# Two banks for the last expert's two halves, and the order lists of a fused attention, gMLP and MoE kernel rewritten

## The chip, the cores and the metric

One core of one Trainium2 chip runs the whole program. The metric is the device time of one execution in microseconds (us); every time below is of that kind or read from one profiled execution. Engines are called as in the profile: PE multiplies matrices (PEld is its loading of weights), DVE is the vector engine, ACT the scalar engine, POOL the general engine, SP the engine that issues most of the transfers.

## What is computed

Three stages, each on the output of the one before, in float32:

```python
# 1. attention, 8 heads, S = 768, D = 64: a key is seen by a query of the same LSH bucket only
q_bucket = bits of (q @ proj > 0); k_bucket = bits of (k @ proj > 0)      # 6 bits
scores = where(q_bucket == k_bucket, q @ k.T / sqrt(D), -1e9)
attn = exp(scores - max); attn = attn / (sum(attn) + 1e-9); out = attn @ v
# 2. gMLP on x [768, 512], d_ff = 1024
h = gelu(x @ w_in); u, v = halves of h
v_n = (v - mu) / sqrt(var + 1e-6) * g_ln
x = x + (u * (w_sg @ v_n + b_sg)) @ w_out
# 3. sticky mixture of 8 experts: each token goes to one expert, its own best one
#    or, where a gate says so, that of the token before
out[s] = p[e] * (relu(x[s] @ w1[e]) @ w2[e])                              # 512 -> 1024 -> 512
```

## The kernel before, in words

**One program, four lists.** The order of every engine's work is written out by hand. Four texts hold it: `ATTENTION` (563 entries), `FEED_FORWARD` (133), `MIXING` (447) and `EXPERTS` (366). `_order` (L165) splits a text into entries of a name and numbers, "*2" meaning twice. A loop over each list (L653, L975, L1029, L1150) calls the step that the name stands for, and each step issues its instructions on its engines. So the place of an entry sets, for each engine that it uses, what stands ahead of it in that engine's queue; an engine takes its queue in order, and a wait at its head holds up all that is behind.

**ATTENTION.** The steps for a head h and a query tile i: `score` (PE, L456 and L459: q times k, and the penalty of the buckets), `max` (DVE, L463), `exp` (ACT, L467), `turn` (PE transposes 128x128 blocks of the numerators, L474), `ev` (ACT copies them to SBUF as `pt`, L480), `pv` (PE, `po<-pt,vt`, L490). `fetch`, `prep` (POOL L404, L405, L215; DVE L398, L384), `project` (PE L440) and `bits` (DVE L447, L449) make q, k and buckets of a head two or one ahead; `prep` also sends pieces through SP (`b<-q`, L399). `vt 0` issues the transfer of all of v into `vt` from ACT's queue (L638); `sum_v` and `pv` read it. `conv` and, later, `cv` are one chunk each of a conversion of the weights w_in and w_out from 64-bit words (`f64_chunks`, `cv_a`, `cv_w`).

**FEED_FORWARD.** `h n t` multiplies row tile t of x with half n of w_in (12 matmuls, L317); n = 1 is the half v. `sq`, `cub`, `tanh`, `gelu` (ACT L753, L757; DVE L755, L764) make the gelu; for the v half `dev`, `var`, `z`, `norm` (DVE L767, L772, L774; ACT L769, L777; POOL `rstd`, L775) make the layer norm, and `vh`, `vl` split it into a high and a low part `vn` (DVE L779, POOL L215). `wsg t i` reads a slice of w_sg (i = 2, SP), casts it (i = 0, ACT `wshi`, L791) and splits off the low part (i = 1, POOL `wslo`, L215, three instructions).

**MIXING.** `mix t k` are the multiplies of w_sg with `vn` for row tile t (L800), `gated` and `gT` and `out` the product with u and w_out; `res` adds the residual, `route` and `half`, `fill`, `rows` the routing. A copy into `route_bank` (DVE L987, ACT L988) stands at one place among them. Beside them run the reads of the experts' weights: 64 parts of 512 KB. `wr` issues the next read (SP, L700), `wh` casts it (ACT, L708), `wl` takes the difference as a low part (DVE, L718; POOL, L215, for 17 of the parts). Six tiles form the ring of the reads, so a read waits for the cast and the split of the part six before it.

**EXPERTS.** For each expert e: `g` and `gx` gather its tokens, `f` multiplies with w1 (L1078), `relu`, `ht` (turns), `y e j` with w2 (L1110, four matmuls per entry), `yo` weighs the sum with the token's probability (`weigh`, DVE L1118, or ACT L1120 for the last two experts), and `send` scatters the rows to the output (`scatter`, POOL, L1123). Experts 0 to 6 have a `y` of 512 columns in six entries. The last has its columns in two halves of six entries each (`cols_of`, L1099), so that the first half can be weighed while the second is multiplied. The sums of expert e lie in PSUM bank "m" or "v", in turn. `ext` (L1131) counts tokens that are left over.

Of the kernel before, what the change touches and what calls it, by code (L numbers as in the profile page):

```python
# [42 lines left out]
ev 1 0, prep 0 k1, prep 0 k2, sum_v 0 1, max 1 1, score 1 3, turn 1 3, exp 1 1, turn 0 6, project 1, sum 1 2,
max 1 3, ev 1 3, sum 1 0, sum_v 0 2, exp 1 3, bits 1 1, turn 1 1, score 1 4, bits 1 2, conv 0, score 1 5, ev 0 6,
sum_v 0 3, max 1 5, sum_v 0 4, sum_v 0 5, turn 1 4, ev 1 1, max 1 4, prep 1 q2, exp 1 5, exp 1 4, bits 1 0,
turn 1 2, ev 1 2, ev 1 4, fetch 2, pv 0 0, pv 0 1, conv 0, pv 0 2, pv 0 3, bits 1 3, sum 1 1, pv 0 4, score 2 0,
max 2 0, turn 1 5, score 2 1, turn 1 7, max 2 1, ev 1 5, exp 2 0, ev 1 7, mean_v 0, prep 1 lo, prep 1 k1, turn 1 8,
score 2 2, prep 1 k2, turn 1 6, exp 2 1, max 2 2, pv 0 5, score 2 3, ev 1 8, zt 0, conv 0, ev 1 6, turn 2 2,
exp 2 2, project 2, turn 2 3, ev 2 2, score 2 4, out 1, turn 2 1, max 2 3, bits 2 1, exp 2 3, ev 2 3, score 2 5,
turn 2 0, ev 2 1, max 2 4, sum 2 1, turn 2 5, conv 0, pv 1 0, ev 2 0, max 2 5, sum 2 0, conv 0, bits 2 2, pv 1 1,  # L50
bits 2 0, prep 2 q2, exp 2 4, ev 2 5, sum 1 3, pv 1 2, turn 2 4, bits 2 3, score 3 0, conv 0, max 3 0, exp 2 5,
score 3 1, max 3 1, prep 2 lo, turn 2 7, ev 2 4, mean 2, sum 3 0, sum 2 2, pv 1 3, fetch 3, pv 1 4, conv 0, ev 2 7,
turn 2 8, conv 0 *2, exp 3 0, score 3 3, turn 2 6, pv 1 5, exp 3 1, prep 2 k1, ev 2 8, conv 0, sum 2 3, ev 2 6,
prep 2 k2, max 3 3, out 2, fetch 4, exp 3 3, sum 3 1, to_x 2, score 3 2, turn 3 0, turn 3 1, mean 3, ev 3 0,
max 3 2, to_x 3, score 3 4, ev 3 1, exp 3 2, conv 0, max 3 4, turn 3 2, turn 3 5, project 3, score 3 5, pv 2 0,
ev 3 5, bits 3 2, pv 2 1, max 3 5, ev 3 2, bits 3 1, conv 0, pv 2 2, turn 3 4, exp 3 4, sum 3 2, exp 3 5, ev 3 4,
bits 3 0, prep 3 k1, turn 3 3, bits 3 3, sum 3 3, conv 0, score 4 0, prep 3 k2, sum 4 1, ev 3 3, turn 3 8, max 4 0,
turn 3 6, score 4 1, conv 0, ev 3 8, ev 3 6, conv 0, xT 3, exp 4 0, pv 2 3, prep 3 q2, pv 2 4, pv 2 5, max 4 1,
exp 4 1, low 3, score 4 2, turn 3 7, mean 4, sum 4 0, max 4 2, turn 4 0, out 3, prep 3 lo, to_x 4, ev 3 7, sum 4 2,
score 4 3, turn 4 2, ev 4 0, exp 4 2, conv 0, turn 4 1, project 4, score 4 4, max 4 3, conv 0, sum 4 3, exp 4 3,  # L60
bits 4 2, score 4 5, bits 4 0, bits 4 3, ev 4 2, turn 4 3, ev 4 1, max 4 4, tri 0, ev 4 3, bits 4 1, turn 4 4,
pv 3 0, max 4 5, pv 3 1, exp 4 4, pv 3 2, score 5 0, ev 4 4, exp 4 5, prep 4 k1, mean 5, prep 4 q2, xT 4, sum 5 1,
turn 4 5, turn 4 6, ev 4 6, max 5 0, score 5 1, prep 4 lo, pv 3 3, pv 3 4, max 5 1, conv 0, ev 4 5, pv 3 5, exp 5 0,
low 4, prep 4 k2, exp 5 1, turn 5 0, turn 4 8, out 4, score 5 2, max 5 2, conv 0, ev 5 0, to_x 5, ev 4 8, turn 4 7,
conv 0, sum 5 0, score 5 3, turn 5 1, project 5, max 5 3, conv 0, ev 4 7, exp 5 2, bits 5 2, fetch 5, score 5 4,
exp 5 3, conv 0, turn 5 2, score 5 5, ev 5 1, turn 5 3, pv 4 0, max 5 4, exp 5 4, bits 5 1, pv 4 1, ev 5 2,
bits 5 0, ev 5 3, conv 0, pv 4 2, max 5 5, turn 5 5, turn 5 4, conv 0, sum 5 2, score 6 0, exp 5 5, bits 5 3,
conv 0, ev 5 4, ev 5 5, conv 0, score 6 1, sum 6 0, sum 6 1, sum 5 3, turn 5 7, turn 5 6, conv 0, prep 5 q2, conv 0,
pv 4 3, pv 4 4, max 6 0, ev 5 7, exp 6 0, prep 5 k1, prep 5 lo, ev 5 6, pv 4 5, max 6 1, conv 0, exp 6 1, prep 5 k2,
score 6 2, xT 5, max 6 2, score 6 5, turn 5 8, conv 0, turn 6 1, conv 0, low 5, out 5, mean 6, pv 5 0, exp 6 2,  # L70
max 6 5, ev 5 8, pv 5 1, to_x 6, score 6 4, exp 6 5, conv 0, turn 6 2, score 6 3, conv 0, ev 6 1, ev 6 2, turn 6 3,
turn 6 0, project 6, pv 5 2, max 6 4, conv 0, max 6 3, bits 6 3, ev 6 0, bits 6 0, exp 6 4, bits 6 2, ev 6 3,
bits 6 1, conv 0, pv 5 3, exp 6 3, turn 6 7, turn 6 8, sum 7 2, sum 7 1, ev 6 7, conv 0, score 7 1, turn 6 4,
max 7 1, conv 0, score 7 0, max 7 0, pv 5 4, ev 6 8, ev 6 4, sum 7 0, exp 7 1, pv 5 5, score 7 4, conv 0, exp 7 0,
out 6, turn 6 5, conv 0, turn 6 6, conv 0, score 7 3, ev 6 5, sum 6 2, prep -1 hi, turn 7 0, max 7 4, sum 6 3,
conv 0, ev 6 6, sum 7 3, conv 0, exp 7 4, xT 6, conv 0, max 7 3, pv 6 0, pv 6 1, exp 7 3, score 7 2, ev 7 0,
max 7 2, score 7 5, turn 7 1, turn 7 2, pv 6 2, conv 0, ev 7 1, exp 7 2, ev 7 2, pv 6 3, conv 0, max 7 5, low 6,
pv 6 4, conv 0, exp 7 5, pv 6 5, turn 7 4, ev 7 4, mean 7, turn 7 7, conv 0, ev 7 7, conv 0, hv 0 0, sum 8 0,
turn 7 3, ev 7 3, conv 0, turn 7 6, hv 2 0, conv 0, ev 7 6, turn 7 8, conv 0, to_x 7, turn 7 5, mean 8, out 7,
sum 8 1, conv 0, ev 7 8, hv 0 1, conv 0, sum 8 2, hv 1 0, conv 0, ev 7 5, to_x 8, xT 7, low 7, pv 7 0, conv 0,  # L80
pv 7 1, conv 0 *2, pv 7 2, conv 0, sum 8 3, pv 7 3, pv 7 4, pv 7 5, conv 0, out 8, hv 3 0, conv 0, mean 9, xT 8,
to_x 9, hv 2 1, hv 1 1, conv 0, hv 0 2, xT 10, hv 1 2, low 8, xT 9, conv 0, hv 3 1, low 10, hv 2 2, hv 3 2, low 9
# [1229 lines left out]
```

## Time and profile before

| | us |
|---|---|
| runs | 343.32, 345.90, 342.52; median 343.32 |
| profiled execution, its own time | 342.49 |
| its span, first to last instruction | 340.7 |
| ATTENTION, to the last `po` | 136.4 |
| first multiply of `mix` | 167.9 |

A run's time has the profiled execution's span and about 1.8 us around it. Busy time is the time in which an engine worked on an instruction. A wait in square brackets in the timeline is the idle time of that engine just before the row's first instruction, with the work that ended it. Rows that follow one another with the same names are joined, with their count behind x.

### The profile page before, as it was taken

What the parts mean: (1) busy time and instruction counts of PE and PEld (TensorE: products, weight loads), DVE (VectorE), ACT (ScalarE), POOL (GpSimd) and SP (SyncE); (2) the same over time, 40 slices, a digit from 0 to 9 for tenths busy, and PEclk for the clock granted to TensorE, in tenths of its full rate; (3) what the DMA queues carried; (4) which work ended last, traced back from release to release, by engine and by line L of the source; (5) the groups of instructions that cost most, each with busy time, mean ns of one, the idle gap of its engine ahead of it and who ended that gap; (6) DMA issues with size and microseconds to landing.
All of it is one profiled execution on the core that took longest, in us unless ns stands there. A gap on an engine that the chain in (4) does not pass through costs nothing.

```text
span 340.7 us, 5610 instructions
## 1 busy us (share of the span) xinstructions
PE 323.5 (95%) x1842; PEld 253.9 (75%) x1842; DVE 263.9 (77%) x524; ACT 228.0 (67%) x403; POOL 216.9 (64%) x314
## 2 busy tenths in 40 slices
...
GB/s 239 52 327 144 196 70 200 117 69 64 202 68 86 64 62 141 63 160 10 2 169 109 201 108 300 158 188 231 360 252 333 350 350 313 285 341 315 282 29 31
DMA packets 27777, 59.97 MB, mean 176 GB/s; under 512 B 3230, under 2 KB 8094, under 8 KB 27744
## 3 DMA queue, kind: packets, MB, share of 16 engines
...
q0 software_dynamic: 1120, 3.15, 2.5%
...
## 4 chain that ended last, share of the span: by engine, by line
PE 39%; DVE 21%; DMA 18%; POOL 10%; issue 7%; ACT 2%; POOLq 1%; DVEq 0%; ACTq 0%
DMA out<-y,dst_row 12%; PE vs L800 7%; PE po L490 6%; DMA raw<-in_w 6%; PE t L474 4%; PE o L823 4%; DVE nb_all L463 3%; PE hv L317 3%; PE eh L1078 3%; POOL q L405 2%; PE s L456 2%; PE s L459 2%; DVE w L718 2%; POOL b L215 2%; POOL r L404 2%
## 5 line engine op out<-in xcount | busy, mean ns | idle before, releaser
L215 POOL TENSOR_TENSOR w<-raw,w 128x256 fp32r<-128x256 f32 x68 | 51.9, 796 | 35.1 <-ACT w L708 35.1
L708 ACT CAST w<-raw 128x1024 fp32r<-128x1024 f32 x64 | 65.4, 1055 | 12.4 <-DMA raw<-in_w 7.8
L718 DVE TENSOR_TENSOR w<-raw,w 128x1024 fp32r<-128x1024 f32 x47 | 57.1, 1253 | 5.1 <-ACT w L708 5.0
L467 ACT ACTIVATE e<-s,nb_all 128x768 f32<-128x768 f32 x48 | 43.5, 907 | 19.1 <-DVE nb_all L463 17.8
L463 DVE TENSOR_REDUCE nb_all<-s 128x1 f32<-128x768 f32 x48 | 45.5, 953 | 9.5 <-PE s L459 8.8
L480 ACT COPY pt<-t 128x512 f32<-128x512 f32 x72 | 40.3, 588 | 10.5 <-PE t L474 10.1
L474 PE MATMUL t<-ident,e 128*128 128x128 f32 x288 | 39.8, 274 | 0.5 <-ACT pt L480 0.4
L474 PEld LDWEIGHTS t<-ident,e 128*128 128x128 f32 x288 | 33.7, 140 | 7.0 <-issue 2.3
L490 PE MATMUL po<-pt,vt 128*64 128x384 f32 x192 | 34.7, 495 | 0.0
L1110 PE MATMUL y<-w,hh 128*128 128x512 f32 (+1 forms) x144 | 33.5, 371 | 0.6 <-ACT y L1120 0.6
L456 PE MATMUL s<-k,q 128*128 128x384 f32 x96 | 28.2, 374 | 0.9 <-ACT e L467 0.9
L1110 PEld LDWEIGHTS y<-w,hh 128*128 128x128 f32 x144 | 24.6, 188 | 4.9 <-ACT y L1120 0.8
L800 PE MATMUL vs<-vn,wshi 128*128 128x512 f32 x72 | 24.9, 407 | 1.9 <-ACT wshi L791 1.9
L459 PE MATMUL s<-k,q 76*128 76x384 f32 x96 | 25.5, 344 | 1.1 <-DVE q L447 0.8
L1123 POOL DMA_INDIRECT out<-y,dst_row x8 | 10.1, 1262 | 25.3 <-DVE y L1118 11.9
L1078 PE MATMUL eh<-w,xh 128*128 128x512 f32 x96 | 24.8, 397 | 0.1
L490 PEld LDWEIGHTS po<-pt,vt 128*64 128x64 f32 x192 | 12.3, 136 | 14.3 <-issue 14.1
L215 POOL TENSOR_TENSOR b<-r,k 64x256 fp32r<-64x256 f32 x21 | 15.9, 784 | 9.9 <-DVE k L384 9.8
L317 PE MATMUL h<-w_in_s,xTs 128*128 128x512 f32 x96 | 22.1, 389 | 0.0
L317 PEld LDWEIGHTS h<-w_in_s,xTs 128*128 128x128 f32 x96 | 18.0, 188 | 3.7
L1078 PEld LDWEIGHTS eh<-w,xh 128*128 128x128 f32 x96 | 17.6, 188 | 4.0 <-DVE w L718 0.5
L456 PEld LDWEIGHTS s<-k,q 128*128 128x128 f32 x96 | 15.0, 189 | 6.5 <-ACT e L467 5.8
...
## 6 DMA issues: line engine op xcount, KB each, us to landing
raw<-in_w SPq DMA_DIRECT2D x64, 512.0 KB, 5.5
...
raw<-in_w_in SPq DMA_DIRECT2D x8, 512.0 KB, 4.0
...
raw<-in_w_out SPq DMA_DIRECT2D x4, 512.0 KB, 4.9
vt<-in_v_tok ACTq DMA_DIRECT2D x1, 1536.0 KB, 11.6
...
```

Of the source, the lines that this page charges most:

```text
L215: nc.gpsimd.tensor_tensor(out[at], a[at], b[at], op=op)
L317: nc.tensor.matmul(ps, a[:, kc, ts_], w_in_s[:, b, kc, ns], start=(kc == 0 and i == 0), stop=(kc == 3 and i == 2))
L456: nc.tensor.matmul(s[:, j, :HALF], q1[:, ts_], k1[:, j * HALF:(j + 1) * HALF], start=True, stop=False)
L463: nc.vector.tensor_reduce(nb_all[:, h, t:t + 1], ss[h, t][:, :, :HALF], axis=AX.XY, op=ALU.max, negate=True)
L467: nc.scalar.activation(e, ss.pop((h, t))[:, :, :HALF], AF.Exp, bias=nb_all[:, h, t:t + 1], accum_out=rs_all[:, h, t:t + 1])
L474: nc.tensor.transpose(ps[:, j * P:(j + 1) * P], es[h, t].rearrange("p g q -> p (g q)")[:, k * P:(k + 1) * P], ident)
L490: nc.tensor.matmul(po[j * D:(j + 1) * D, :HALF], vt[:, kt, h * D:(h + 1) * D], pt.rearrange("p (t k) q -> p k t q", k=NT)[:, kt, j * 3:(j ...
L708: nc.scalar.copy(slabs_of[i, e][:, 0, q * 2:(q + 1) * 2, :], raws[part])
L718: nc.vector.tensor_tensor(lo, raw, hi, op=ALU.subtract)
L800: nc.tensor.matmul(ps, a[:, kc, :], b[:, kc, :], start=(k == 0), stop=(k == 17))
L1078: nc.tensor.matmul(ps[e, n], a[:, kc, :], slabs_of[1, e][:, b, kc * 2 + n, :], start=(k == 0), stop=(k == 11))
L1110: nc.tensor.matmul(yb[e][:, cs], a[:, kc, :], slabs_of[2, e][:, b, kc, cs], start=(k == 0), stop=(k == 23))
```

## The change

It has two parts.

**Banks.** `second` (L1102) keys the bank by the expert and the half, and takes "m" or "v" by the sum of the two numbers. For experts 0 to 6 nothing changes. The last expert's first half stays in "v", and its second half goes to "m". `weigh` (L1112) reads the bank of its own half.

```diff
         def second(e, j):
-            if e not in yb:
-                yb[e] = bank("mv"[e % 2], f"y{e}")
+            part = (e, j // 6)
+            if part not in yb:
+                yb[part] = bank("mv"[(e + j // 6) % 2], f"y{e}_{j // 6}")
             hh, hl = hx[e]
...
-                nc.tensor.matmul(yb[e][:, cs], a[:, kc, :], slabs_of[2, e][:, b, kc, cs], start=(k == 0), stop=(k == 23))
+                nc.tensor.matmul(yb[part][:, cs], a[:, kc, :], slabs_of[2, e][:, b, kc, cs], start=(k == 0), stop=(k == 23))
...
-                nc.vector.tensor_scalar(ys[e][:, cs], yb[e][:, cs], prob[:, e:e + 1], None, op0=ALU.mult)
+                nc.vector.tensor_scalar(ys[e][:, cs], yb[e, j][:, cs], prob[:, e:e + 1], None, op0=ALU.mult)
...
-                nc.scalar.activation(ys[e][:, cs], yb[e][:, cs], AF.Copy, scale=prob[:, e:e + 1])
+                nc.scalar.activation(ys[e][:, cs], yb[e, j][:, cs], AF.Copy, scale=prob[:, e:e + 1])
```

**Lists.** Each list holds the same entries as before, in another order. Against its list, the place of an entry changes for 529 of 563 in ATTENTION, 126 of 133 in FEED_FORWARD, 420 of 447 in MIXING and 336 of 366 in EXPERTS, by 7, 4, 6 and 5 places in the median. The list of MIXING is a line shorter, so lines after it count one less up to `cols_of`. Of the lists two lines are enough, the last of EXPERTS:

```diff
-y 7 3, ht 7 1 2, ext 0, y 7 4, y 7 5, send 6 0, y 7 6, y 7 7, yo 7 0, y 7 8, y 7 9, y 7 10, y 7 11
+yo 7 0, y 7 6, y 7 7, y 7 8, y 7 9, y 7 10, y 7 11, send 6 0
```

In FEED_FORWARD the last six `h` entries were `h 1 4`, `h 0 1`, `h 0 4`, `h 0 2`, `h 0 5`, `h 0 3`; they are now `h 0 4`, `h 0 3`, `h 1 4`, `h 0 2`, `h 0 5` behind `h 1 5`. Three places follow as the engines have them.

PE at the end of EXPERTS, before; `y_3811` is the last expert's sum, `hh` and `hl` the high and low part of its turned relu, `pc` the count of `ext`:

```order
L1110 MATMUL y_3811<-w_7_3752,hh 128x256 x16
...
L1131 MATMUL pc<-ohb_all,ones_b 128x8
L1110 MATMUL y_3811<-w_7_3752,hl 128x256 x8
L1110 MATMUL y_3811<-w_7_3752,hh 128x256 x16
L1110 MATMUL y_3811<-w_7_3752,hl 128x256 x8
```

and in the new kernel:

```order
L1110 MATMUL y_0_3818<-w_7_3755,hh 128x256 x16
...
L1131 MATMUL pc<-ohb_all,ones_b 128x8
L1110 MATMUL y_0_3818<-w_7_3755,hl 128x256 x8
L1110 MATMUL y_1_3884<-w_7_3755,hh 128x256 x16
L1110 MATMUL y_1_3884<-w_7_3755,hl 128x256 x8
```

The order of the matmuls stays; the second half has a tile of its own, `y_1`.

PE in the opening, before; `s` are scores of head 1, `t` its turns, `pj` the projection of head 2, `po` the product of head 0 with v:

```order
L456 MATMUL s_1_369<-k_1_184,q_1_183 128x384 x2
L459 MATMUL s_1_369<-k_1_108,q_1_185 128x384 x2
L474 MATMUL t_0_374<-ident,e_0_356 128x128 x4
L456 MATMUL s_3_389<-k_1_184,q_1_183 128x384 x2
L459 MATMUL s_3_389<-k_1_108,q_1_185 128x384 x2
L474 MATMUL t_3_394<-ident,e_2_360 128x128 x4
L474 MATMUL t_6_401<-ident,e_4_333 128x128 x4
L440 MATMUL pj_406<-k_2_304,wz 108x384
...
L474 MATMUL t_2_466<-ident,e_1_399 128x128 x4
L490 MATMUL po_475<-pt_238,vt 64x384 x10
```

and in the new kernel:

```order
L455 MATMUL s_1_362<-k_1_195,q_1_194 128x384 x2
L458 MATMUL s_1_362<-k_1_108,q_1_196 128x384 x2
L473 MATMUL t_0_379<-ident,e_0_350 128x128 x4
L489 MATMUL po_392<-pt_232,vt 64x384 x2
L455 MATMUL s_3_395<-k_1_195,q_1_194 128x384 x2
L458 MATMUL s_3_395<-k_1_108,q_1_196 128x384 x2
L439 MATMUL pj_410<-k_2_306,wz 108x384
```

The first two matmuls of `po` stand ahead of the last score of the group and of the projection; before, all of the first ten stood behind them and behind further turns and scores.

POOL from FEED_FORWARD into MIXING, before; `rstd` is the layer norm's factor, `vn` the low part of the normed v, `wslo` a slice of w_sg's low part, `cv_w` and `w_out_s` pieces of the conversion of w_out:

```order
L775 TENSOR_TENSOR rstd<-var,eps_1739 128x1
L215 TENSOR_TENSOR vn<-z,vn 128x256 x2
L775 TENSOR_TENSOR rstd<-var,eps_1739 128x1
L215 TENSOR_TENSOR w_out_s<-cv_w,w_out_s 128x256 x2
L215 TENSOR_TENSOR wslo<-wsr,wshi 128x256 x3
L215 TENSOR_TENSOR vn<-z,vn 128x256 x4
L215 TENSOR_TENSOR cv_w<-cv_w,cv_a 128x256 x2
L215 TENSOR_TENSOR wslo<-wsr,wshi 128x256 x3
```

and in the new kernel:

```order
L214 TENSOR_TENSOR wslo<-wsr,wshi 128x256 x3
L214 TENSOR_TENSOR vn<-z,vn 128x256 x2
L214 TENSOR_TENSOR cv_w<-cv_w,cv_a 128x256 x2
L214 TENSOR_TENSOR vn<-z,vn 128x256 x2
L774 TENSOR_TENSOR rstd<-var,eps_1739 128x1 x2
L214 TENSOR_TENSOR w_out_s<-cv_w,w_out_s 128x256 x2
L214 TENSOR_TENSOR vn<-z,vn 128x256 x4
L214 TENSOR_TENSOR cv_w<-cv_w,cv_a 128x256 x2
L214 TENSOR_TENSOR wslo<-wsr,wshi 128x256 x3
```

The second `wslo` stands ahead of two `vn` pairs and two `rstd`; the four `vn`, `cv_w` and the third `wslo` behind them follow one another in both.

## Rows read from the trace of the kernel before

**Rows 1.** The page: busy time by engine; the weight reads among the transfers.
```profile
PE 323.5 (95%) x1842; PEld 253.9 (75%) x1842; DVE 263.9 (77%) x524; ACT 228.0 (67%) x403; POOL 216.9 (64%) x314
...
raw<-in_w SPq DMA_DIRECT2D x64, 512.0 KB, 5.5
```
**Rows 2.** Windows: stretch, length, busy (count) of PE, PEld, DVE, ACT, POOL, clock, DMA share, GB/s.
```profile
0.00:20.00 20.00, 15.87 (x92) 13.26 (x93) 13.75 (x26) 9.91 (x19) 8.60 (x20) 1.00 0.55 167
...
160.00:180.00 20.00, 17.64 (x73) 13.10 (x73) 18.12 (x32) 12.16 (x23) 17.25 (x22) 1.00 0.20 73
...
220.00:240.00 20.00, 18.55 (x135) 15.66 (x133) 17.89 (x82) 11.12 (x21) 14.44 (x19) 1.00 0.69 235
240.00:260.00 20.00, 20.00 (x101) 16.57 (x100) 13.88 (x16) 14.10 (x19) 6.92 (x8) 1.00 0.85 303
260.00:280.00 20.00, 20.00 (x100) 16.51 (x99) 15.34 (x16) 15.71 (x21) 8.46 (x10) 1.00 0.98 353
...
320.00:341.00 21.00, 13.66 (x91) 11.97 (x89) 8.39 (x29) 6.52 (x10) 7.51 (x9) 0.95 0.13 49
...
sum 341.00, PE 323.53 PEld 253.91 DVE 263.89 ACT 227.96 POOL 216.93; mean PE 17.97 PEld 14.11 DVE 14.66 ACT 12.66 POOL 12.05
```
**Rows 3.** Waits of PE: who waited for whom, us in total, times, longest.
```profile
PE vs L800 <- ACT wshi L791: 1.9, 1, 1.9
...
PE route_bank L878 <- ACT x2t L839: 0.7, 1, 0.7
...
PE t L474 <- ACT pt L480: 0.4, 1, 0.4
```
**Rows 4.** Timeline of the end: start, us, engine, line, operation, output and inputs, count, wait.
```profile
323.86 3.18 POOL L215 TENSOR_TENSOR w<-raw,w 128x256 fp32r<-128x256 f32 x4 [0.91 <-ACT w L708]
...
327.19 2.14 PE L1110 MATMUL y<-w,hh 128*128 128x256 f32 x16
327.95 0.69 ACT L1120 ACTIVATE y<-y,prob 128x512 f32<-128x512 f32 x1
...
330.25 1.03 PEld L1110 LDWEIGHTS y<-w,hh 128*128 128x128 f32 x8
...
331.61 0.47 ACT L1120 ACTIVATE y<-y,prob 128x256 f32<-128x256 f32 x1 [2.96 <-PE y L1110]
332.13 1.00 PEld L1110 LDWEIGHTS y<-w,hh 128*128 128x128 f32 x8 [0.85 <-ACT y L1120]
332.14 1.21 PE L1110 MATMUL y<-w,hh 128*128 128x256 f32 x8 [0.65 <-ACT y L1120]
```
**Rows 5.** The tile `vt`: time from its issue to its landing.
```profile
DMA to landing us min/median/max: 11.6/11.6/11.6
```
**Rows 6.** Timeline of the opening.
```profile
13.26 1.02 DVE L398 TENSOR_SCALAR q<-r 128x768 fp32r<-128x768 f32 x1
...
16.62 0.39 ACTq L638 DMA_DIRECT2D vt<-in_v_tok  x1
...
26.49 0.62 PE L456 MATMUL s<-k,q 128*128 128x384 f32 x2
...
29.19 0.40 PE L440 MATMUL pj<-b,wb 128*108 128x384 f32 x1 [0.50 <-DMA b<-q]
...
40.71 0.61 PE L456 MATMUL s<-k,q 128*128 128x384 f32 x2 [0.41 <-ACT e L467]
```
**Rows 7.** Timeline from FEED_FORWARD to MIXING.
```profile
156.64 11.27 PE L317 MATMUL h<-w_in_s,xTs 128*128 128x512 f32 x49
...
168.99 2.76 POOL L215 TENSOR_TENSOR wslo<-wsr,wshi 128x256 fp32r<-128x256 f32 x3
...
170.22 0.73 PE L800 MATMUL vs<-vn,wslo 128*128 128x512 f32 x2 [0.44 <-POOL wslo L215]
...
171.71 3.90 POOL L215 TENSOR_TENSOR vn<-z,vn 128x256 fp32r<-128x256 f32 x4
...
179.03 0.96 PE L800 MATMUL vs<-vn,wshi 128*128 128x512 f32 x3 [1.92 <-ACT wshi L791]
```

More of the change, by code (lines that the diff above doesn't have):

```diff
@@ L43 @@
[L43 to L82, printed above, removed]
+warm 0 6, conv 0, prep -1 k1, score 0 1, warm 0 12, score 0 2, turn 0 0, prep -1 q2, max 0 1, exp 0 1, ev 0 0,
@@ new lines @@
+prep 1 k2, sum 1 3, turn 1 6, out 1, score 2 4, turn 2 1, mean 2, conv 0, max 2 3, sum 2 0, exp 2 3, ev 1 6,
+project 2, score 2 5, turn 2 4, pv 1 0, max 2 4, bits 2 0, exp 2 4, ev 2 1, pv 1 1, sum 2 2, conv 0, pv 1 2,
+max 2 5, ev 2 4, turn 2 5, bits 2 1, bits 2 2, exp 2 5, ev 2 5, score 3 0, conv 0, prep 2 k1, prep 2 q2, zt 0,
+conv 0, sum 3 0, turn 2 6, score 3 1, max 3 0, turn 2 3, conv 0, prep 2 k2, pv 1 3, ev 2 3, sum 3 1, exp 3 0,
+pv 1 4, pv 1 5, bits 2 3, max 3 1, ev 2 6, score 3 3, prep 2 lo, conv 0, out 2, conv 0, sum 3 2, turn 2 7, max 3 3,
@@ new lines @@
+to_x 2, exp 3 1, ev 2 7, turn 2 8, score 3 2, turn 3 2, ev 2 8, sum 2 3, mean 3, exp 3 3, max 3 2, turn 3 1, to_x 3,
+score 3 4, max 3 4, ev 3 2, conv 0, ev 3 1, exp 3 2, turn 3 5, project 3, turn 3 0, bits 3 1, score 3 5, bits 3 2,
+pv 2 0, sum 3 3, pv 2 1, conv 0, fetch 3, conv 0, fetch 4, bits 3 0, ev 3 0, max 3 5, pv 2 2, exp 3 4, conv 0,
+prep 3 q2, ev 3 5, exp 3 5, bits 3 3, prep 3 k1, turn 3 3, conv 0, ev 3 3, turn 3 4, score 4 0, max 4 0, ev 3 4,
+conv 0, xT 3, turn 3 7, exp 4 0, score 4 1, turn 3 8, max 4 1, pv 2 3, pv 2 4, sum 4 1, low 3, tri 0, pv 2 5,
@@ new lines @@
+ev 3 7, score 4 2, prep 3 k2, prep 3 lo, turn 3 6, mean 4, exp 4 1, conv 0, max 4 2, ev 3 8, turn 4 1, out 3,
+to_x 4, score 4 3, ev 3 6, exp 4 2, ev 4 1, max 4 3, turn 4 0, exp 4 3, project 4, sum 4 0, score 4 5, turn 4 4,
+conv 0, score 4 4, ev 4 0, conv 0, turn 4 2, sum 4 2, ev 4 4, sum 4 3, max 4 5, turn 4 3, fetch 5, pv 3 0, bits 4 1,
+prep 4 k1, max 4 4, pv 3 1, pv 3 2, mean 5, conv 0, bits 4 0, exp 4 5, bits 4 2, ev 4 2, score 5 0, prep 4 q2,
+conv 0, turn 4 5, ev 4 3, bits 4 3, prep 4 k2, exp 4 4, score 5 1, turn 4 6, max 5 0, prep 4 lo, conv 0, xT 4,
@@ new lines @@
+pv 3 3, pv 3 4, pv 3 5, exp 5 0, conv 0, score 5 2, max 5 1, sum 5 1, low 4, max 5 2, prep -1 hi, ev 4 6, ev 4 5,
+out 4, exp 5 1, conv 0, turn 4 7, to_x 5, turn 4 8, ev 4 7, score 5 3, conv 0, exp 5 2, max 5 3, conv 0, sum 5 0,
+turn 5 0, ev 5 0, ev 4 8, project 5, bits 5 0, score 5 5, sum 5 2, max 5 5, turn 5 1, sum 5 3, turn 5 3, exp 5 3,
+exp 5 5, score 5 4, pv 4 0, pv 4 1, conv 0, prep 5 k1, ev 5 1, turn 5 2, conv 0, ev 5 3, bits 5 1, bits 5 2, ev 5 2,
+bits 5 3, turn 5 4, score 6 0, max 5 4, turn 5 5, prep 5 k2, ev 5 4, prep 5 q2, exp 5 4, conv 0, ev 5 5, max 6 0,
```

160 lines of the change are left out of this document (89 added, 71 removed).

## The prediction

> **What bounds the kernel now.** I read four views. First the page's head with the windows: PE is busy for 323.5 us, 95% of the span [rows 1], and the table by stretch says where it is not [rows 2]. In windows that add up to 341.00 us PE idles 341.00 − 323.53 = 17.47 us: 20.00 − 15.87 = 4.13 before 20 us, 21.00 − 13.66 = 7.34 after 320 us, and so 6.0 us in the 300 us between, of which 160 to 180 us has 20.00 − 17.64 = 2.36 and 220 to 240 us has 1.45. From 240 us to 320 us PE never stops. So PE's own work sets the time; a new order can win only what is left of those 6.0 us and a part of the two ends, and it can lose wherever it makes PE wait.
>
> Second, PE's waits by releaser [rows 3]: among those after the opening, the longest is for the cast of a w_sg slice (`wshi`), 1.9 us. Third, the timeline at the places where the change moves something: the end [rows 4], the opening with the landing of `vt` [rows 5, 6], and the step from FEED_FORWARD to MIXING [rows 7]. I looked last at the weight stream of the experts: one kind of read, 64 of 512 KB [rows 1], holds the transfer engines at 0.98 of their time with 353 GB/s in 260 to 280 us [rows 2].
>
> The sum is made against the profiled execution, 342.49 us; it stands 0.83 under the median of the three runs, 343.32, and by the fastest of them, 342.52.
>
> **The end.** In before, both halves of the last expert's `y` lie in one bank. PE has loaded the last weights of the first half by 330.25 + 1.03 = 331.28; ACT weighs that half at 331.61 for 0.47; only then does PE load the next weights, 0.85 idle, and multiply, 0.65 idle [rows 4]. In the new kernel the second half goes to bank "m", out of which ACT has weighed the expert before by 327.95 + 0.69 = 328.64 [rows 4], and the ACT step stands beside PE's second half. What covers it: the first eight of the second half's multiplies alone take PE 1.21, the ACT step 0.47. No other instruction is added; the chain behind it (second half, ACT, scatter) keeps its length, so the whole wait comes off the time. Its size is 0.65 by the multiply's row and 0.85 by the weight load's. I take 0.85, from that 331.28 to the next load at 332.13, since a load marks where PE resumed.
>
> The Trainium skill ("Perfetto Trace Analysis", § Tensor Engine Instruction (MATMUL, LD_WEIGHTS)) says that the profiler estimates the end of a multiply from its size, so that its end is a model; by that rule the 0.65 is the less sure of the two readings, and this trace has the two 0.2 us apart. By the 0.65 the sum would come out 0.2 higher.
>
> **The opening.** The new list puts `pv 0 0` right behind `turn 1 0`, ahead of `score 1 3` and `project 1`; before, `pv 0 0` stands behind these two and seven more tiles of turns and scores. `pv` needs `vt`, which ACT's queue issues at 16.62 [rows 6] and which lands 11.6 us later [rows 5], at 28.2. PE is at that place when `turn 1 0` is done, before the next score tile, which begins at 26.49 [rows 6]. So PE would wait 28.22 − 26.49 = 1.73 us, with everything of PE queued behind it: score 1 3, the projection of head 2, the next turns. That also delays DVE (`max 1 3`) and ACT (`exp 1 3`). The issue itself may come later: DVE now does the 1.02 of `prep q2` [rows 6] ahead of `max 0 1` and not behind it, and `exp 0 3`, behind which `vt` is issued, follows DVE; if 0.8 of the 1.02 comes through, the wait is 2.5. Against it: the projection's wait of 0.50 for `b` at 29.19 [rows 6] and a score's wait for ACT, 0.41 at 40.71 [rows 6], are over by the time PE arrives. That leaves 1.73 − 0.91 = +0.8 or 2.5 − 0.91 = +1.6; if `vt` lands 1.4 sooner it is 0.3 − 0.91 = −0.6. I take the middle, +0.5, between −0.6 and +1.6.
>
> **From FEED_FORWARD to MIXING.** Two things. On POOL the second `wslo` split (three instructions, 2.76 us, at 168.99) moves from behind two `rstd`, four `vn` and two `w_out_s` to ahead of them, so the wait of 0.44 that PE has for it at 170.22 [rows 7] goes. But `h 1 4`, third from last among the `h` tiles in the new list and sixth from last before, starts the chain of the v half of row 4 (gelu, mean, variance, norm, `vh`, `vl`) later, by up to three tiles of 12 multiplies at 11.27 / 49 = 0.23 us [rows 7], 8.3 us. That chain ends in POOL's four `vn` (171.71, 3.90); behind them POOL has `cv_w`, which DVE's own `cv_w` takes up; DVE's queue has that ahead of a bank copy that ACT waits for, and only behind this stands ACT's cast `wshi`, for which PE waits 1.92 [rows 7]. The new list keeps that order (the four `vn`, `cv_w`, then the third `wslo`), so this wait stays. Its bounds: all the idle time of this stretch goes, −2.36 [rows 2]; or the chain ends one tile of `h` later, 12 × 0.23 = 2.76, less the 0.44: +2.3. Before, POOL's `wslo` ends at 168.99 + 2.76 = 171.75, just where the four `vn` begin [rows 7]; with that split out of the way they can begin as soon as their inputs stand, and part of what the later `h` costs is paid by this. I take +0.3 on the 1.92 and −0.44 for `wslo`: −0.1 in all, nearest to the rows as they stand.
>
> **Elsewhere.** The rest of ATTENTION and the route steps of MIXING move a handful of places with the same multiset of work; PE has 1.45 idle in 220 to 240 us [rows 2], which bounds what can go. I cost it at nothing: work by the same instructions, PE without a gap on both sides. In EXPERTS nothing can be won before 320 us, as PE is busy for all of it; what it costs if the cover goes is the slower rival below.
>
> Sum: 342.49 − 0.85 + 0.5 − 0.1 = 342.04, so 342.0 us.
>
> **The rivals.** *Faster: the new order removes most of the waits inside.* The largest after 20 us are 1.9 (`wshi`), 0.7 (`route_bank`), 0.5 (`b`), 0.4 (`wslo`) and 0.4 (`pt`) [rows 3, 6, 7], 3.9 together; with the end, 342.49 − 3.9 − 0.85 = 337.7. For it: each of these is a wait on another engine's place in its list, and all five lie where lists changed. Against it: the new `pv` wait, and the unchanged order in front of `wshi`.
>
> *Slower: the weight stream comes late.* A read goes into one of six ring tiles and waits until that tile has been cast (`wh`) and split (`wl`). In the new MIXING some of this is listed later against PE's work: of its 180 `mix` and `out` entries, 125 stood ahead of the sixth split and 140 do now, 131 ahead of the eighth read and 162 now. So reads can start later in 200 to 240 us. If they stand one ring later, that is six parts of 512 KB, 3.1 MB at 353 GB/s, 8.9 us. The stream can make up 0.15 × 20 = 3.0 us in 240 to 260 us, and nothing after it, where the share is 0.98 [rows 2]. At the end the last POOL split is done at 323.86 + 3.18 = 327.04 and is needed from the thirteenth of the sixteen multiplies that begin at 327.19, at 327.19 + 12/16 × 2.14 = 328.8: 1.75 of lead [rows 4]. So PE loses 8.9 − 3.0 − 1.75 = 4.15, or 5.9 if the lead is gone too: 345.8 to 347.5 with the end's 0.85 off; I take 346.6 between them. It decides once reads slip by more than 4.75 us. Against it: both lists have 18 reads, 12 casts and 12 splits done by the end of MIXING, and the transfers had room there, 0.69 in 220 to 240 us [rows 2].
>
> The Trainium skill ("HBM Reference", § Specifications (TRN2)) gives a core that streams alone about 425 GB/s. By that figure the slip of 3.1 MB would be made up in 7.4 us and this rival would be an estimated 1.5 cheaper. The trace speaks against it: at a share of 0.98 the engines moved 353 [rows 2].
>
> *The two banks bring nothing*, as bank "m" is not free in time or the scatter behind the end is bound otherwise: 342.49 + 0.5 − 0.1 = 342.9.
>
> **How the numbers follow.** Forecast 0.54, faster rival 0.23, late stream 0.17, no gain at the end 0.06. The forecast's own range, from its bounds taken together in part, is 339.5 to 344.5. The range of 8 in 10 reaches to the faster rival's 337.7 and nearly to 346.6: 338.0 to 346.4. A measurement of this kernel can tell about 1%, 3.4 us, from no change. Faster by more than that: all of the rival but the part near the line, 0.20, and 0.04 of the forecast; slower: 0.15 of the late stream and 0.01 of the forecast's high end; the rest, 0.60, within.
>
> **What would show it.** At the end no wait of PE for ACT's `y`. Near 27 to 29 us a wait of PE's first `po` for the DMA of `vt`, of 1 to 2.5 us. No wait for `wslo` at the first `vs` tiles, and one for `wshi` of 1 to 3 us at `mix 2 0`. In 240 to 320 us PE busy throughout. The forecast is wrong if PE waits there for `w` (late stream), or if `wshi`'s wait is gone and the end of ATTENTION comes over 1 us sooner (faster rival).

## The result

The changed kernel is slower by 0.8%: median 346.2 us of 22 runs against 342.65 of 22, ratio 1.0081 with the 95% interval 1.0055 to 1.0107, which is +2.8 us. Medians, here and below, are of all runs of a kernel, while the ratios leave out runs over 1.5% above the fastest of their kernel, so the two can differ. I had forecast 342.0 and a ratio a little under 1. The time lies at the high end of the range that I gave, 346.4, and on the other side of no change.

Two executions of the changed kernel were traced, of 355.08 and 345.99 us; the rows below are of the second, with a span of 344.2. This is a part of its table by stretch, with the columns of [rows 2]:

```profile
20.00:40.00 20.00, 18.20 (x112) 14.93 (x111) 14.61 (x22) 12.36 (x26) 15.04 (x26) 0.91 0.68 195
...
220.00:240.00 20.00, 19.07 (x132) 16.60 (x131) 16.89 (x81) 11.38 (x22) 18.23 (x25) 0.91 0.76 264
...
260.00:280.00 20.00, 18.49 (x90) 15.08 (x89) 16.60 (x18) 14.92 (x19) 4.83 (x6) 1.00 0.99 364
```

Two things are new against [rows 2]. In 260 to 280 us, where PE never stopped before, it is idle for 1.5 us and runs 90 multiplies instead of 100. And the granted clock is 0.91 in two stretches, 20 to 40 and 220 to 240 us, where it was 1.00. The waits of PE, with the columns of [rows 3]:

```profile
PE vs L799 <- ACT wshi L790: 2.0, 1, 2.0
PE po L489 <- DMA vt<-in_v_tok: 1.5, 1, 1.5
PE xgT L1063 <- DMA xg<-xd,src_row: 1.5, 1, 1.5
...
PE hT L1088 <- ACT hs L1082: 1.0, 2, 0.8
```

`wshi` waits as before. The wait for `vt` is the one that I had expected. The gather `xg` and the last expert's relu `hs` are waits of EXPERTS that were not there. At the end, which answers to [rows 4], the last expert's second half follows the first without a wait:

```profile
333.30 1.01 PEld L1110 LDWEIGHTS y<-w,hl 128*128 128x128 f32 x8
...
334.23 1.99 PEld L1110 LDWEIGHTS y<-w,hh 128*128 128x128 f32 x16
...
334.35 2.08 PE L1110 MATMUL y<-w,hh 128*128 128x256 f32 x16
...
334.63 0.47 ACT L1120 ACTIVATE y<-y,prob 128x256 f32<-128x256 f32 x1 [2.50 <-PE y L1110]
```

The sixteen loads from 334.23 on are the second half's; before, they stood in two rows of eight, at 330.25 and 332.13, with ACT's step between them [rows 4]. Nothing parts them any more, and ACT's step at 334.63 stands beside them. So the end does what was forecast. Still, the last `y` begins its last eight multiplies at 336.27 and not at 333.19.

### The profile page after: what moved, and what is told of

Its sections match the earlier page's. It is cut to its first block, busy times and chain, and to the rows that moved or that the text cites. A ratio compares the mean times of both kernels' runs of the same rounds, so it can differ in the third digit from the quotient of the medians.

```text
span 353.2 us, 5600 instructions
## 1 busy us (share of the span) xinstructions
PE 329.6 (93%) x1842; PEld 260.2 (74%) x1842; DVE 262.9 (74%) x524; ACT 228.3 (65%) x403; POOL 217.7 (62%) x314
## 4 chain that ended last, share of the span: by engine, by line
PE 49%; DMA 21%; DVE 15%; issue 6%; POOL 3%; ACT 3%; POOLq 0%; DVEq 0%; ACTq 0%
DMA out<-y,dst_row 10%; PE po L489 9%; PE t L473 8%; PE vs L799 6%; PE s L455 4%; PE s L458 4%; DMA vt<-in_v_tok 4%; DMA raw<-in_w 4%; PE o L822 3%; PE eh L1077 3%; PE hv L316 3%; PE y L1110 2%; DMA xg<-xd,src_row 2%; PE pj L439 2%; DVE w L717 2%
## 5 line engine op out<-in xcount | busy, mean ns | idle before, releaser
L214 POOL TENSOR_TENSOR w<-raw,w 128x256 fp32r<-128x256 f32 x68 | 53.0, 813 | 41.1 <-ACT w L707 41.1
L717 DVE TENSOR_TENSOR w<-raw,w 128x1024 fp32r<-128x1024 f32 x47 | 59.6, 1306 | 6.4 <-ACT w L707 6.3
L473 PE MATMUL t<-ident,e 128*128 128x128 f32 x288 | 41.1, 274 | 0.0
L1110 PE MATMUL y<-w,hh 128*128 128x512 f32 (+1 forms) x144 | 34.8, 381 | 2.3 <-POOL w L214 2.3
L455 PE MATMUL s<-k,q 128*128 128x384 f32 x96 | 29.1, 385 | 0.4 <-ACT e L466 0.4
L799 PE MATMUL vs<-vn,wshi 128*128 128x512 f32 x72 | 26.3, 418 | 2.7 <-ACT wshi L790 2.0
L1077 PE MATMUL eh<-w,xh 128*128 128x512 f32 x96 | 25.7, 402 | 0.1
L214 POOL TENSOR_TENSOR cv_w<-cv_w,cv_a 128x256 f32<-128x256 f32 x24 | 18.1, 774 | 5.7 <-DVE cv_w L287 3.3
L214 POOL TENSOR_TENSOR wslo<-wsr,wshi 128x256 fp32r<-128x256 f32 x18 | 13.9, 804 | 11.5 <-ACT wshi L790 11.5
```

The costliest lines, as they stand in the source:

```text
L214: nc.gpsimd.tensor_tensor(out[at], a[at], b[at], op=op)
L455: nc.tensor.matmul(s[:, j, :HALF], q1[:, ts_], k1[:, j * HALF:(j + 1) * HALF], start=True, stop=False)
L473: nc.tensor.transpose(ps[:, j * P:(j + 1) * P], es[h, t].rearrange("p g q -> p (g q)")[:, k * P:(k + 1) * P], ident)
L717: nc.vector.tensor_tensor(lo, raw, hi, op=ALU.subtract)
L799: nc.tensor.matmul(ps, a[:, kc, :], b[:, kc, :], start=(k == 0), stop=(k == 17))
L1077: nc.tensor.matmul(ps[e, n], a[:, kc, :], slabs_of[1, e][:, b, kc * 2 + n, :], start=(k == 0), stop=(k == 11))
```

## The experiments

I started with two theories. Theory 1: the loss is made in the opening, by the wait for `vt` and the lower clock behind it. Theory 2: it is made by the weight stream in the experts. Four kernels tell them apart. Ratios are to the kernel before on the same chip.

**The changed kernel once more** (no edit).

> The changed kernel once more, for a trace of it that is not disturbed. Theory 1 (the opening): the first po waits 2 to 3.5 us for the transfer of vt, the granted clock is at its lower level for a few us behind that wait, and the last po of the attention ends 2 to 3 us later than the 136.4 of before, at about 139; the loss is made there. Theory 2 (the weight stream): the last po ends within 1 us of 136.4, and the loss appears behind 240 us as waits of PE for w. Both: ratio to before near 1.008.

Measured: 346.24 us, ratio 1.0046 (1.0002 to 1.0090). The last `po` ends at 132.45 + 4.09 = 136.5, against 132.26 + 4.09 = 136.4 before. Theory 1's 139 is not there, although the wait for `vt` is, and a lower clock behind it.

**The two banks alone**, on the lists of before: the diff of the code above and nothing else.

> The kernel before with the two banks alone, its own four lists. Both theories: PE's wait of 0.85 (weight loads) or 0.65 (multiplies) for ACT's y at the end is gone and nothing else changes, 342.65 - 0.85 = 341.8, ratio 0.9975. If the second bank brings nothing at the end: ratio 1.000.

Measured: 341.88 us, ratio 0.9989 (0.9954 to 1.0024). The wait is gone, as the timeline shows; the loads follow one another at 329.56 + 1.01 = 330.57:

```profile
329.56 1.01 PEld L1111 LDWEIGHTS y<-w,hl 128*128 128x128 f32 x8
...
330.50 1.99 PEld L1111 LDWEIGHTS y<-w,hh 128*128 128x128 f32 x16
```

0.85 us is 0.25%, which the interval holds beside nothing at all: the mechanism is shown by the rows, its worth in time is not.

**Banks and the new ATTENTION**, the other three lists as before.

> The kernel before with the two banks and the new ATTENTION list alone. Theory 1: 341.8 and about 3 for the wait for vt and the lower clock behind it, 344.8, ratio 1.006, last po at about 139. Theory 2: 341.8 within 0.5, ratio 0.996 to 0.999, as the weight stream's lists are those of before.

Measured: 339.75 us, ratio 0.9916 (0.9884 to 0.9948). Both theories miss: the new ATTENTION is not the loss, it wins, some 2.5 us against the banks alone. It does so with the wait for `vt` in it, 1.8 us in its trace, and a lower clock behind that.

**pv 0 0 moved back**, in the changed kernel:

```diff
-turn 1 0, bits 0 3, prep 0 k2, max 1 1, fetch 2, pv 0 0, score 1 3, sum 1 2, ev 1 0, max 1 3, exp 1 1, exp 1 3,
+turn 1 0, bits 0 3, prep 0 k2, max 1 1, fetch 2, score 1 3, sum 1 2, ev 1 0, max 1 3, exp 1 1, exp 1 3,
...
-sum_v 0 3, ev 1 1, sum_v 0 4, turn 1 4, max 1 5, ev 1 4, bits 1 1, pv 0 1, sum 1 0, conv 0, pv 0 2, bits 1 0,
+sum_v 0 3, ev 1 1, sum_v 0 4, turn 1 4, max 1 5, ev 1 4, bits 1 1, pv 0 0, pv 0 1, sum 1 0, conv 0, pv 0 2, bits 1 0,
```

> The changed kernel with the one entry pv 0 0 moved back to just ahead of pv 0 1, so that the first po stands behind turns, scores and the projection again, all else as changed. Theory 1: no wait for vt, no lower clock in the opening, 345.4 - 3 = 342.4, ratio 0.999. Theory 2: the loss stays, 345.4, ratio 1.008.

Measured: 346.73 us, ratio 1.0069 (1.0017 to 1.0121). The last `po` ends at 130.10 + 3.72 = 133.8, 2.7 us sooner than in the trace above, so there the wait and the clock behind it did cost that much. The time does not show it: 2.7 us would be 0.8%, and the ratio is 0.1% lower. Theory 1 falls. What is lost is lost behind the attention.

In the traces of both kernels PE waits for a gather near 262 us, and near 328 us for ACT. So I formed two theories on what stands behind the attention: E, the order of EXPERTS, and M, MIXING's later reads (the rival of the prediction). Three kernels add one new list each to the banks and the new ATTENTION (339.75), and a fourth undoes one thing in the changed kernel.

**With the new EXPERTS:**

> Two banks, the new ATTENTION and the new EXPERTS, FEED_FORWARD and MIXING as before. Base: the same without the new EXPERTS, 339.75. Theory E (the loss is in the order of EXPERTS: expert 4's gather has no buffer until expert 2's tokens are turned and lands late, 1.5 to 1.9; casts and relu of the last expert late, 1.0 to 1.6): PE waits for the gather in front of an xgT tile near 262 us and the time is 343 to 344.5. Theory M (the new MIXING starts the weight reads later): 339.75 within 0.7.

Measured: 346.47 us, ratio 1.0085 (1.0044 to 1.0126). Theory E's sign, and more than its size: +1.7%, 5.8 us.

**With the new MIXING:**

> Two banks, the new ATTENTION and the new MIXING, FEED_FORWARD and EXPERTS as before. Base 339.75. Theory M: the reads 8 to 13 come 7 to 10 us later, the stream stays late, and PE waits for w or for ACT near the end, 342 to 344.5. Theory E: the stream has caught up by 265 us, 339.75 within 0.7.

Measured: 341.35 us, ratio 0.9937 (0.9901 to 0.9973). Theory M falls: PE has no wait for w behind 240 us, and the ratio lies within the interval of the base. The reads are later for a while, as I had read from the list (the ninth begins at 213.8 against 208.1 in the base), but the 29th begins at 258.0 against 258.9.

**With the new FEED_FORWARD:**

> Two banks, the new ATTENTION and the new FEED_FORWARD, MIXING and EXPERTS as before. Base 339.75. Both theories: within 0.7 of it; the wait for wslo of 0.5 goes, that for wshi stays at 1.5 to 2.5. If the late h 1 4 costs what I bounded at most, 342.

Measured: 340.92 us, ratio 0.9927 (0.9888 to 0.9966). As expected, no difference that can be told. The wait for `wslo` is gone, that for `wshi` is 2.6.

**g 4 and g 5 swapped**, in the changed kernel's EXPERTS:

```diff
-... gx 1 1, g 5, f 0 0 1,
+... gx 1 1, g 4, f 0 0 1,
...
-... wh 0, g 4, xt 4 0, ...
+... wh 0, g 5, xt 4 0, ...
```

> The changed kernel with two entries swapped, g 4 and g 5, so that expert 4's tokens are gathered early and expert 5's later. Theory E: PE's wait of 1.5 to 1.9 for the gather near 262 us is gone, and with it the lower clock that follows it in some runs: 346.2 - 1.5 to - 3.5, 342.7 to 344.7. Theory M: the stream of weights is what is late, PE waits for it elsewhere, 346.2 within 1.

Measured: 345.65 us, ratio 1.0100 (1.0049 to 1.0152), from six runs. The wait for the gather is gone from the trace. Whether the time is better can't be told: two runs took 339.79 (the traced one) and 342.62, four took 345.25 to 347.72 at a lower granted clock (0.982 to 0.987 against 0.996 and 0.992), and the two alone would give 0.997. The swap does not bring the gain reliably, so what follows the gather is worth a look. The trace with the new EXPERTS shows what that is. First PE's rows with a wait behind 240 us (the last part of a row is the wait):

```profile
257.97 0.63 PE L1064 MATMUL xgT<-ident,xg 128*128 128x128 f32 x4 [1.80 <-DMA xg<-xd,src_row]
...
295.73 2.11 PE L1078 MATMUL eh<-w,xh 128*128 128x512 f32 x8 [0.18 <-ACT xh L1067]
...
319.27 1.20 PE L1111 MATMUL y<-w,hh 128*128 128x512 f32 x4 [1.39 <-ACT hh L1095]
...
327.12 0.51 PE L1111 MATMUL y<-w,hh 128*128 128x512 f32 x1 [2.33 <-POOL w L215]
```

Then POOL in the same trace, the scatters (L1124) and the weight splits (L215) from 286 us on:

```profile
289.61 2.83 POOL L215 TENSOR_TENSOR w<-raw,w 128x256 fp32r<-128x256 f32 x4 [2.46 <-ACT w L708]
299.06 0.99 POOL L1124 DMA_INDIRECT out<-y,dst_row  x1 [6.62 <-DVE y L1119]
305.63 0.97 POOL L1124 DMA_INDIRECT out<-y,dst_row  x1 [5.58 <-DMA out<-y,dst_row]
306.62 5.89 POOL L215 TENSOR_TENSOR w<-raw,w 128x256 fp32r<-128x256 f32 x4
312.67 1.79 POOL L1124 DMA_INDIRECT out<-y,dst_row  x1 [0.16 <-issue]
322.30 4.76 POOL L215 TENSOR_TENSOR w<-raw,w 128x256 fp32r<-128x256 f32 x4 [7.84 <-ACT w L708]
```

Read from the top: POOL has done the split of expert 4 at 292.4 and stands before `send 3`, which the new list puts ahead of `send 2`. Expert 3's sum is weighed late, so POOL waits 6.62. Then comes `send 2`, whose sum has long been ready; both scatters write `out`, and it waits 5.58 for the first to land. Only at 306.62 does POOL start the split of expert 5's last part, whose tile in the ring the read six parts later needs: the split ends at 306.62 + 5.89 = 312.51, and that read, the seventh from the end, is issued at 312.54. With it the last seven reads come late, and so does the next split, at 322.30, for which PE waits 2.33 until 327.12. The same place with the EXPERTS of before (banks and the new ATTENTION):

```profile
295.01 1.80 POOL L1124 DMA_INDIRECT out<-y,dst_row  x1 [0.16 <-issue]
303.29 1.72 POOL L1124 DMA_INDIRECT out<-y,dst_row  x1 [6.48 <-DVE hl L1097]
305.59 4.55 POOL L215 TENSOR_TENSOR w<-raw,w 128x256 fp32r<-128x256 f32 x4 [0.58 <-ACT w L708]
```

There `send 2` is out at 295.01, over 4 us before expert 3's sum is weighed (DVE ends that at 299.46). `send 3` follows at 303.29, the rest of its wait being, as I read it, for `send 2` to land: so the wait for the sum and the wait for the landing overlap, while with the new list one follows the other. The split waits for its own cast alone, 0.58. The SP rows give what that does to the reads: the last seven begin at 312.54 with the new EXPERTS and at 310.17 without, though in its trace the kernel with the new EXPERTS is 4.4 us ahead when the experts begin (first `eh` at 231.29 against 235.73); counted from there they are 6.8 us late. With the new EXPERTS first, then without (x7, the last seven):

```profile
312.54 7.85 SPq L700 DMA_DIRECT2D raw<-in_w  x7
```
```profile
310.17 7.61 SPq L700 DMA_DIRECT2D raw<-in_w  x7
```

This is theory S, with theory C (casts and splits late by their own order) as its rival.

**send 2 and send 3 swapped**, in the changed kernel:

```diff
-y 4 1, wr 0, wl 0, f 6 1 1, ht 5 0 0, y 4 2, wr 0, y 4 3, yo 3 0, ht 4 0 2, f 6 1 2, wl 0, send 3 0, wh 0, wl 0,
-wr 0, send 2 0, ht 5 0 1, y 4 4,
+y 4 1, wr 0, wl 0, f 6 1 1, ht 5 0 0, y 4 2, wr 0, y 4 3, yo 3 0, ht 4 0 2, f 6 1 2, wl 0, send 2 0, wh 0, wl 0,
+wr 0, send 3 0, ht 5 0 1, y 4 4,
```

> The changed kernel with two entries of EXPERTS swapped, send 3 and send 2, so that the scatters of experts 2 and 3 are issued in the order in which their sums are ready. Theory S (in the new list POOL waits for expert 3's sum and then 5 to 6 us for that scatter to land before it may issue the next, and the weight split queued behind holds back a ring tile and so the last reads): the split for expert 5's last part starts 3 to 4 us sooner against its cast, PE's waits for w and for casts behind 315 us are gone, 346.2 - 2 to - 4, 342.2 to 344.2, with the gather's wait left. Theory C (the last reads are late by the order of casts and splits, whatever POOL's scatters do): 346.2 within 1.

Measured: 345.23 us, ratio 1.0013 (0.9958 to 1.0068). In its trace the split starts 2.1 us sooner than in the changed kernel, where theory S had 3 to 4, and PE has no wait for w or for the relu behind 300 us. First the changed kernel's row, then this one's:

```profile
309.58 3.85 POOL L214 TENSOR_TENSOR w<-raw,w 128x256 fp32r<-128x256 f32 x4
```
```profile
307.48 3.88 POOL L214 TENSOR_TENSOR w<-raw,w 128x256 fp32r<-128x256 f32 x4
```

In time it points the way of theory S, but its interval overlaps that of the changed kernel.

**Both pairs swapped:**

> The changed kernel with both pairs swapped: send 3 with send 2, and g 4 with g 5. Theory S and E together: no wait for the gather, none for w at the end, 346.2 - 5 to - 6.5, 339.7 to 341.2, and a granted clock near that of the kernel before. Theory C: 344 to 346.

Measured: 340.84 us, ratio 0.9948 (0.9913 to 0.9982). Four entries of some 1500 turn the changed kernel from slower to faster than before; against 1.0081 that is −1.3%, 4.6 us, more than the whole loss. One pair alone does not bring this reliably: 11 of these 12 runs are under 344 us, against 2 of 6 with the gathers alone swapped and 2 of 12 with the sends alone. POOL and the last seven reads now:

```profile
294.54 1.50 POOL L1123 DMA_INDIRECT out<-y,dst_row  x1 [2.01 <-DVE w L717]
302.51 1.05 POOL L1123 DMA_INDIRECT out<-y,dst_row  x1 [6.46 <-ACT w L707]
303.57 3.87 POOL L214 TENSOR_TENSOR w<-raw,w 128x256 fp32r<-128x256 f32 x4
```
```profile
307.47 8.48 SPq L699 DMA_DIRECT2D raw<-in_w  x7
```

No PE row behind 240 us shows a wait. Theory C falls with it, as the order of casts and splits is that of the changed kernel.

What the sends are worth where the gather is already right can be read from two traces, as the one with the gathers swapped alone begins the experts at the same time as this one. The first `eh` and the last row of `y`, gathers alone and then both pairs:

```profile
232.01 2.09 PE L1077 MATMUL eh<-w,gxhi 128*128 128x512 f32 x8
...
331.97 1.12 PE L1110 MATMUL y<-w,hl 128*128 128x256 f32 x8
```
```profile
232.09 2.09 PE L1077 MATMUL eh<-w,gxhi 128*128 128x512 f32 x8
...
330.77 1.12 PE L1110 MATMUL y<-w,hl 128*128 128x256 f32 x8
```

That is 1.2 us, just the two waits for the last relu (0.42 and 0.78) that the trace with the gathers alone still has. Neither trace has a drop of the clock before its last `y`; where a wait brings one, it costs more.

**pv 0 0 moved back, on two bases.** First on the banks and the new ATTENTION, then on the changed kernel with both pairs swapped.

> Two banks and the new ATTENTION, with pv 0 0 moved back to pv 0 1, the other three lists as before. Base, without the move: 339.75. If what the wait for vt and the lower clock behind it cost in the attention (its last po at 133.1 and not 135.8) comes through to the end: 337.0 to 337.5. If the weight stream of the experts takes it back: 339.75 within 0.7.

Measured: 339.05 us, ratio 0.9881 (0.9833 to 0.9929), the fastest kernel of the study. The last `po` ends at 130.43 + 4.09 = 134.5, 2.0 sooner than without the move. Against 0.9916 the gain of 0.35% is within the intervals: it can't be told whether it comes through.

> The changed kernel with both pairs swapped and pv 0 0 moved back. Theory S and E, and the opening's cost coming through: 337 to 339. If the stream of the experts takes the opening's gain back: as with both pairs alone, 339.7 to 341.2. Theory C: 344 to 346.

Measured: 341.41 us, ratio 0.9968 (0.9929 to 1.0007), no better than without the move. Its trace shows no gain in the opening that could arrive: the last `po` ends at 134.4, and at 134.0 without the move, where PE waited only 0.68 for `vt` and the clock did not fall. Why that differs from the 2.7 above is told in the next section.

**EXPERTS out of the changed kernel, and alone in the kernel before.**

> The changed kernel with the EXPERTS list of before: banks, ATTENTION, FEED_FORWARD and MIXING new. If the loss is in EXPERTS alone: 339.75 to 341.5, as with the new ATTENTION alone, PE without a wait for the gather and for w behind 240 us. If FEED_FORWARD and MIXING together bring a loss that neither has alone: 343 and more.

Measured: 343.02 us, ratio 1.0010 (0.9979 to 1.0042). Without the new EXPERTS the loss of 0.8% is gone, but the 0.9916 of the new ATTENTION alone is not reached: FEED_FORWARD and MIXING together cost 0.9%, 3 us, though each alone lay within the intervals (0.9927 and 0.9937). The two alone add up to 0.3%, but with four intervals of some 0.35% each in the comparison, it can't be told that together they cost more than their sum. Its trace has one wait that the base lacks, PE's at the start of the experts:

```profile
235.76 1.16 PE L1077 MATMUL eh<-w,gxhi 128*128 128x512 f32 x4 [1.41 <-DVE dst_row L946]
```

The new MIXING alone has it with 1.04. Smaller waits come to it: from the first `vs` to the last `y` the trace takes 168.1 us with PE idle for 6.2, while the base takes 167.4, idle for 4.1, of which 1.7 went to one drop of the clock. So some 2.4 of the 3 us stand in this trace, which at 339.75 us is the shortest of its kernel's runs. Over the runs that the ratios compare, (1 − granted clock) × span, an estimate of what the clock takes, is 3.8 us against 2.7 in the base. That about covers the rest; what brings the clock down there I have not followed.

> The kernel before with the two banks and the new EXPERTS alone. If the order of EXPERTS loses by itself, whatever stands ahead of it: 341.9 + 4 to + 6.7, 346 to 348.5, with the wait for the gather and waits at the end. If it needs the new ATTENTION, FEED_FORWARD or MIXING ahead of it: 341.9 within 1.5.

Measured: 345.82 us, ratio 1.0113 (1.0064 to 1.0163), +1.2% or 4.2 us against the banks alone. The order of EXPERTS loses by itself, with the wait for the gather and the one for w. Its timeline, PE and POOL:

```profile
262.86 0.63 PE L1064 MATMUL xgT<-ident,xg 128*128 128x128 f32 x4 [1.46 <-DMA xg<-xd,src_row]
...
330.21 0.50 PE L1111 MATMUL y<-w,hh 128*128 128x512 f32 x1 [2.28 <-POOL w L215]
```
```profile
303.93 0.99 POOL L1124 DMA_INDIRECT out<-y,dst_row  x1 [6.81 <-DVE y L1119]
309.50 0.97 POOL L1124 DMA_INDIRECT out<-y,dst_row  x1 [4.57 <-ACT w L708]
310.48 4.85 POOL L215 TENSOR_TENSOR w<-raw,w 128x256 fp32r<-128x256 f32 x4
```

`send 2` is named as released by ACT's `w` here. I take it for the landing of the scatter before, which the other trace names: POOL goes on 5.6 us behind that scatter's start, 6.6 there.

## Why the prediction was wrong, step by step

**EXPERTS: "nothing can be won before 320 us, as PE is busy for all of it" is the step that failed.** I read 80 us without a gap as a stretch in which no order could matter except through MIXING's reads. It was full because its order kept two resources free in time, and the new order does not. One is the third `xg` buffer: `g 5` takes it early, so `g 4` can't be issued before PE has turned expert 2's tokens, and the list has it right ahead of `xt 4 0`. In the trace of the changed kernel, expert 2's turn, POOL, and expert 4's turn:

```profile
249.34 0.60 PE L1063 MATMUL xgT<-ident,xg 128*128 128x128 f32 x4
250.76 3.92 POOL L214 TENSOR_TENSOR w<-raw,w 128x256 fp32r<-128x256 f32 x4 [7.76 <-ACT w L707]
...
254.84 2.05 POOL L1042 DMA_INDIRECT xg<-xd,src_row  x1
...
262.02 0.63 PE L1063 MATMUL xgT<-ident,xg 128*128 128x128 f32 x4 [1.51 <-DMA xg<-xd,src_row]
```

The buffer is free at 249.94, but by the list a weight split stands ahead of the gather on POOL, so it is issued at 254.84, and PE stands before expert 4's turn until 262.02. The other is POOL's queue: `send 3` ahead of `send 2` holds up the split behind them, and by it the last reads. Both stood in the list and in POOL's order, and I looked for neither: I compared where casts, splits and reads stand, and not what else stands on POOL ahead of them, nor how many buffers the gathers have. The size: +1.2% alone, +1.7% behind the new ATTENTION. Waits of 1.5 to 1.9 us for the gather and of up to 2.3 for w make a part of it, and the clock that falls behind some of them another; how the loss divides between the two pairs the runs don't settle.

**The slower rival had the right resource and the wrong place.** It said that the weight stream comes late and PE waits for w at the end, 345.8 to 347.5 us with the end's gain taken off; measured were 346.2 in the median, and in the trace of 355.08 us PE waits 2.27 for w at 336.07; in the one of 345.99 it waits for the last relu. But it blamed MIXING, and MIXING's later reads cost nothing that can be told: the stream had caught up by the 29th read of 64. What it called slack in 240 to 260 us was there. So it is luck that the median lies between its bounds. The chance of 0.17 was too low because the mechanism that holds the last reads was not looked for at the end.

**The end: right in size, one row misread.** −0.85 by the rows; the runs can't tell it from nothing. But the loads from 330.25 on are not the last of the first half: they are the first eight of the second. In the list `yo 7 0` stands behind `y 7 7`, and with both halves in one bank ACT's step waited for those eight multiplies (330.37 + 1.12 = 331.49; ACT at 331.61), and PE then for ACT. With two banks the first of these waits is gone as well.

**The opening: the wait was right, its price not.** Forecast 1.7 to 2.5 us, measured 1.54 in this trace. I did not price what follows it. These are four-microsecond windows of the changed kernel:

```profile
26.00:30.00 4.00, 2.46 (x15) 1.58 (x14) 1.62 (x3) 2.73 (x6) 3.75 (x7) 1.00 0.96 217
30.00:34.00 4.00, 4.00 (x19) 3.80 (x18) 2.85 (x4) 1.02 (x3) 4.00 (x7) 0.57 0.83 267
34.00:38.00 4.00, 4.00 (x29) 2.48 (x27) 3.84 (x8) 3.06 (x7) 3.17 (x6) 1.00 0.01 3
```

PE is idle for 1.5 of the first four; then the granted clock falls to 0.57 of full in the mean, most of it at the lower of its two levels, 1.2 GHz, and PE does 19 multiplies where the next four microseconds have 29. Wait and clock together cost the 2.7 us between 136.5 and 133.8. My sum had +0.5, which took the waits behind it as a cushion and held no clock. The other traces part the two. Ten have `pv 0 0` early, and their wait for `vt` runs from 0.33 to 3.51 us. In six the clock does not fall behind it (waits of 0.33 to 1.87), and the last `po` ends at 133.7 to 135.2; with `pv 0 0` moved back, in three traces, it ends at 133.8 to 134.5. In four it falls (waits of 1.54 to 3.51), and the last `po` ends at 136.5 to 139.4. At nearly the same wait the drop costs 1.9 us (1.54 against 1.45) and 1.3 (1.79 against 1.87). So without a drop the price is about 1 us or less, as the sum had it, and the term that was left out is the clock.

**"The rest of ATTENTION ... I cost it at nothing": wrong by about 2.5 us of gain.** In time the new ATTENTION is worth 0.7%, with the opening's cost inside. Where the clock does not fall in the opening, the last `po` ends 1.2 to 2.7 us sooner than before. I took none of it into the sum, as I had followed no chain of the attention behind the opening, and I gave a reason that does not hold: the same instructions, and PE without a gap. The sum rows of the tables by stretch, from the start up to the first `vs`, in before and then with the new ATTENTION and EXPERTS (no drop of the clock in either):

```profile
sum 167.87, PE 161.61 PEld 123.02 DVE 138.05 ACT 122.12 POOL 119.92; mean PE 53.87 PEld 41.01 DVE 46.02 ACT 40.71 POOL 39.97
```
```profile
sum 164.45, PE 160.22 PEld 123.23 DVE 135.97 ACT 122.16 POOL 119.71; mean PE 53.41 PEld 41.08 DVE 45.32 ACT 40.72 POOL 39.90
```

Of the 3.4 us, 2.0 are idle time of PE and 1.4 are busy time: the same multiplies in another order keep PE busy for less. In the trace with only EXPERTS as before the busy time is 159.7, 2.0 less. So the idle time that I counted is not all that a new order can win. Which neighbours make the multiplies cheaper I have not followed.

**FEED_FORWARD to MIXING: right in its rows, open in time.** The wait for `wslo` is gone, `wshi`'s is 2.00 against the 2.22 (1.92 + 0.3) that I took, and two small ones for `vn`, 0.7 together, are new; −0.1 was forecast. That the two lists together cost 0.9% was not: the routing's wait at the start of the experts (1.41), smaller waits and the clock, as told above, were no terms of the sum.

The sum of the parts as run: banks −0.1%, ATTENTION −0.7%, FEED_FORWARD and MIXING +0.9%, EXPERTS +0.7% on top of the three, together +0.8%. The parts don't add on other bases (EXPERTS costs 1.2% and 1.7% there). That the stream of weights takes back what a stage ahead of it gains is a guess that no run here shows.
